# Linear-attention block and gated FFN on one core: later weights behind the last crossbar transpose, first x tiles and K weight halves in turns, four Q units between the halves of the late Gram chunks

**Chip, core, metric.** One core of one Trainium2 chip. The metric is the device time of one execution in microseconds (us). Every execution lists its time and the span of its records; in all runs here the time is the span + 1.7 us. All runs were in the fast state, with a granted TensorE clock of 0.998 to 1.0. Ratios are the mean time of one kernel's fast runs over the mean of the other's fast runs of the same rounds, so they are not quite the ratio of the medians quoted beside them.

## The reference

```python
def reference(A_x, A_wqkv, A_wo, B_x, B_w_gate, B_w_up, B_w_down):
    # x: 1 x 2048 x 576 bf16; wqkv 576 x 1728; 32 heads of 18; FFN width 4608
    xn = _layernorm(x)                               # (x - mean) / sqrt(var + 1e-5)
    q, k, v = split(xn @ wqkv)
    phi = lambda t: jnp.where(t > 0, t + 1, jnp.exp(t)) + 1e-6
    pq, pk = phi(q), phi(k)
    kv = einsum("bhsd,bhse->bhde", pk, v);  z = einsum("bhsd->bhd", pk)
    o = einsum("bhqd,bhde->bhqe", pq, kv) / (einsum("bhqd,bhd->bhq", pq, z)[..., None] + 1e-6)
    ffn = (gelu(xn @ w_gate) * (xn @ w_up)) @ w_down
    return x + o.reshape(B, S, D) @ wo + ffn
```

## The kernel before

The kernel never forms V. It sums the Gram matrix of phi(K) with the normalised x over all 16 token tiles, and multiplies V's weights by it afterwards. For each tile of 128 tokens: VectorE takes statistics and normalises; tiles 0 to 3 are transposed on TensorE, tiles 4 to 15 by a DMA crossbar transpose; TensorE projects K in two halves of 288 columns; ScalarE and VectorE form phi(K); TensorE adds to the Gram chunks. Q units (one of 5 head chunks by 512 tokens) fill in. Chunks 2 and 3 of the Gram matrix wait until chunks 0, 1 and 4 have left PSUM. The order of each engine is the order of a list of (time, step) pairs.

Some words used below. "K 8" or "Gram 15" is that work for tile 8 or 15. A pass is one instruction of VectorE or ScalarE that reads a matmul's result. A bank is one of the eight parts of PSUM (numbers 0 to 7) that the matmuls write. In a row-paired unit two matmuls of 64 rows each start together. The pitch is the even distance between the starts of two pieces of work when TensorE waits for nothing, here 3.05 us from one tile's K to the next; what goes beyond it is called late by the pitch.

```python
    load_x(0, 1)
    load_x(1, 1)
    load_x(2, 2)          # tiles 2 and 3
    load_w(1)             # K weights, all 576 columns
    load_x(4, 2)
    load_x(6, 2)
    load_w(0)             # Q weights
    ...
    def k_bank(n, hf):
        return hf if n == 1 else 5 + hf          # tile 1's halves stand in PSUM banks 0 and 1
    G_A = {0: [(0, ...), (1, ...)], 1: [(2, ...), (3, ...)], 4: [(0, ...), (1, ...), (2, ...)]}   # bank first
    ...
    loads = [lambda n, i=i: load_gu(i // 2, i % 2) for i in range(2 * NWBUF)]   # gate and up blocks
    loads.insert(1, lambda n: load_w(2, 0, 2))                                  # V weights
    loads.insert(3, lambda n: load_w(2, 2, 4))
    todo += [(18.0 + TILE * i, step, 0) for i, step in enumerate(loads)]        # TILE = 2.94
    ...
    for n in range(NS):                       # NS = 16: behind tile 15's Gram
        g_accumulate(n, {2: G_B[2]})
    g_copy(4, G_A, ...); g_copy(0, G_A, ...); g_copy(1, G_A, ...)
    for _, step, n in todo[tail:]:            # the passes of the last Q units
        step(n)
    q_unit(12); ...
```

## Time and profile before

| | before, first profile | before, profile of the first experiment call |
|---|---|---|
| time of that execution | 526.45 | 525.5 |
| span | 524.7 | 523.8 |
| median of the timed runs | 524.73 (524.69 to 524.99) | 524.96 (524.37 to 525.50) |
| crossbar transposes of tiles 8 and 14, issue to landing | 4.52 and 2.60 | 2.61 and 2.59 |
| Gram 15 starts | 54.85 | 53.78 |
| FFN starts | 73.41 | 72.33 |

"Gram 15 starts" is the point up to which the head runs tile by tile; "FFN starts" is the first gate or up matmul. Both can be found in the timeline of TensorE.

### The profile page before, as it was taken

Reading aid. Unit: us, or ns where it says so; the run is one execution under the profiler, and the core shown is the slowest. Engines: PE = TensorE matmul, PEld = TensorE weight load, DVE = VectorE, ACT = ScalarE, POOL = GpSimd, SP = SyncE. Lnnn points to the kernel's source line nnn. Section 1 sums busy time; section 2 is a strip of 40 time slices with the busy share of each in tenths; the row PEclk is TensorE's granted clock in tenths of the full one; section 3 lists DMA queues with packets and bytes.
Section 4 is the critical chain, followed back from the end, with each engine's and each line's share of the span. In section 5 each row is a group of like instructions: output and inputs, shape, how many; then the busy total and the mean of one; then the engine's idle time right before and its main releaser. Section 6 shows DMA issues by size and latency. Waiting matters only on the chain.

```text
span 524.7 us, 10664 instructions
## 1 busy us (share of the span) xinstructions
PE 517.2 (99%) x4502; PEld 315.8 (60%) x4502; DVE 248.4 (47%) x426; ACT 147.9 (28%) x301; POOL 40.1 (8%) x63
## 2 busy tenths in 40 slices
PE   7999999999999999999999999999999999999997
PEld 7767764555577754444577744444777544445775
DVE  7887545977348423333388134333584233333110
ACT  5989563233230012332200033232000123222000
POOL 2012130121001100000011000000011000000000
PEclk9999999999999999999999999999999999999999
DMA  8565009999500035555300065555100355540000
GB/s 262 135 156 119 1 2 240 264 268 265 169 21 24 12 103 158 158 144 158 108 12 13 28 174 143 156 159 151 32 22 12 104 158 157 144 130 1 12 11 24
DMA packets 106443, 57.90 MB, mean 110 GB/s; under 512 B 13402, under 2 KB 105754, under 8 KB 106394
## 3 DMA queue, kind: packets, MB, share of 16 engines
q1 hardware_dynamic: 106394, 57.21, 38.8%
q8 instruction: 35, 0.57, 0.4%
q14 instruction: 14, 0.11, 0.1%
HBM read 52.86 MB, written 2.36 MB: 105 GB/s over the span
## 4 chain that ended last, share of the span: by engine, by line
PE 96%; DMA 2%; ACT 1%; DVE 0%; SPq 0%; issue 0%; DVEq 0%
PE ps_all L318 55%; PE ps_all L664 27%; PE ps_all L669 4%; PE ps_all L294 3%; PE ps_all L250 3%; PE ps_all L347 3%; DMA wqkv_sb<-in_A_wqkv_dram 1%; DMA xnT<-xn 1%; PE ps_all L442 1%; PE ps_all L424 0%; PE ps_all L646 0%; SPq L93 0%; ACT phi_e L270 0%; DVE hT L278 0%; ACT xnT L239 0%; ACT phi_e L274 0%
## 5 line engine op out<-in xcount | busy, mean ns | idle before, releaser
L318 PE MATMUL ps_all<-xnT,wg 64*128 64x512 bf16 x1152 | 273.0, 376 | 0.0
L318 PE MATMUL ps_all<-xnT,wu 64*128 64x512 bf16 x1152 | 271.6, 376 | 0.0
L635 DVE TENSOR_TENSOR hT<-ps_all,gl 128x512 bf16<-128x512 f32 x144 | 99.4, 691 | 161.2 <-ACT gl L634 160.7
L634 ACT ACTIVATE gl<-ps_all 128x512 f32<-128x512 f32 x144 | 86.0, 598 | 312.7 <-PE ps_all L318 295.8
L318 PEld LDWEIGHTS <-wu 64*128 64x128 bf16 x1152 | 108.1, 94 | 66.0 <-SPq L327 0.7
L318 PEld LDWEIGHTS <-wg 64*128 64x128 bf16 x1152 | 108.1, 94 | 65.7 <-issue 0.5
L664 PE MATMUL ps_all<-wd_sb,hT 128*128 128x288 bf16 x1152 | 147.0, 286 | 0.0
L664 PEld LDWEIGHTS <-hT 128*128 128x128 bf16 x1152 | 112.3, 98 | 30.6 <-issue 1.3
L466 DVE RECIPROCAL den_sb<-den_sb 126x128 f32<-126x128 f32 (+1 forms) x80 | 68.3, 911 | 0.5
L672 DVE TENSOR_TENSOR res<-ps_all,x_sb 128x288 bf16<-128x288 f32 x32 | 14.6, 458 | 88.0 <-PE ps_all L669 88.0
L318 PE MATMUL ps_all<-xnT,wr 64*128 64x512 bf16 x288 | 55.7, 376 | 0.0
L469 POOL TENSOR_TENSOR pqT<-pqT,den_sb 126x512 bf16<-126x512 bf16 (+3 forms) x25 | 24.1, 965 | 299.2 <-DVE den_sb L466 276.0
L669 PE MATMUL ps_all<-m_sb,pqT 126*128 126x288 bf16 (+1 forms) x160 | 24.9, 285 | 0.0
L318 PEld LDWEIGHTS <-wr 64*128 64x128 bf16 x288 | 14.6, 94 | 16.7 <-issue 0.7
L250 PE MATMUL ps_all<-wqkv_sb,xnT 128*128 128x288 bf16 x160 | 22.5, 286 | 1.7 <-DMA wqkv_sb<-in_A_wqkv_dram 0.8
L294 PE MATMUL ps_all<-hT,xn 128*128 128x288 bf16 (+4 forms) x176 | 22.4, 276 | 0.0
L294 PEld LDWEIGHTS <-xn 128*128 128x128 bf16 (+1 forms) x176 | 17.5, 102 | 4.3
L250 PEld LDWEIGHTS <-xnT 128*128 128x128 bf16 x160 | 15.3, 98 | 7.6 <-issue 1.3
L393 DVE SCALAR_TENSOR_TENSOR pqT<-ps_all,phi_e 126x512 bf16<-126x512 f32 (+1 forms) x20 | 13.4, 672 | 12.4 <-POOL phi_e L389 12.4
L669 PEld LDWEIGHTS <-pqT 126*128 126x128 bf16 (+1 forms) x160 | 15.5, 97 | 4.1
L347 PE MATMUL ps_all<-xnT,wqkv_sb 128*126 128x512 bf16 (+1 forms) x70 | 17.4, 378 | 0.0
L389 POOL TENSOR_SCALAR phi_e<-phi_e 126x512 f32<-126x512 f32 (+1 forms) x20 | 12.4, 618 | 54.2 <-DVE hT L278 29.8
(63 smaller groups left out, 183.8 us busy)
## 6 DMA issues: line engine op xcount, KB each, us to landing
wg<-in_B_w_gate_dram SPq DMA_DIRECT2D x72, 256.0 KB, 2.9
wu<-in_B_w_up_dram SPq DMA_DIRECT2D x72, 256.0 KB, 3.5
wd_sb<-in_B_w_down_dram SPq DMA_DIRECT2D x12, 432.0 KB, 4.7
wr<-in_B_w_gate_dram SPq DMA_DIRECT2D x72, 32.0 KB, 2.7
wr<-in_B_w_up_dram SPq DMA_DIRECT2D x72, 32.0 KB, 3.1
out_dram<-res SPq DMA_DIRECT2D x15, 144.0 KB, 1.8
wqkv_sb<-in_A_wqkv_dram SPq DMA_DIRECT2D x2, 576.0 KB, 6.0
x_sb<-in_A_x_dram SPq DMA_DIRECT2D x2, 576.0 KB, 7.2
```

The costliest lines, as they stand in the source:

```text
L250: nc.tensor.matmul(ps_all[:, k_bank(n, hf), :HALF], lhsT=xnT[:, kt, n * P:(n + 1) * P], rhs=wqkv_sb[:, kt, D + hf * HALF:D + (hf + 1) * HALF],
L294: nc.tensor.matmul(ps_all[:m, b, col:col + w], lhsT=xn[:, n, j0:j0 + m], rhs=pk[:, n, d0:d0 + w], start=(n == 0 and col == 0), stop=(n == ...
L318: return nc.tensor.matmul(self.outs[i], lhsT=self.lhs(i, rows, kt), rhs=self.rhs(i, rows, kt), start=start, stop=stop, skip_group_check=True,)
L347: nc.tensor.matmul(ps, lhsT=wqkv_sb[:, kt, q0:q0 + rows], rhs=xnT[:, kt, sc * SC:(sc + 1) * SC], start=(kt == 0), stop=(kt == KT - 1),)
L393: nc.vector.scalar_tensor_tensor(out=out_, in0=ps, scalar=0.0, in1=e, op0=ALU.max, op1=ALU.add)
L466: nc.vector.reciprocal(out=d[:, h:h + P], in_=d[:, h:h + P])
L469: nc.gpsimd.tensor_tensor(out=pqT[:rows, c, cols], in0=pqT[:rows, c, cols], in1=d, op=ALU.mult)
L634: nc.scalar.activation(out=gl[:], in_=ps_all[:, b[0], :], func=ACT.Gelu_apprx_tanh)
L635: nc.vector.tensor_tensor(out=hT[:, GUB * k + i, :], in0=ps_all[:, b[1], :], in1=gl[:], op=ALU.mult)
L664: nc.tensor.matmul(acc, lhsT=hT[:, f, j * P:(j + 1) * P], rhs=wd_sb[:, f, hs], start=(f == 0), stop=False,)
L669: nc.tensor.matmul(acc, lhsT=pqT[:rows, c, ts_], rhs=m_sb[:rows, c, hs], start=False, stop=(c == NCH - 1),)
L672: nc.vector.tensor_tensor(out=res[:, hs], in0=acc, in1=x_sb[:, n, hs], op=ALU.add)
```

## The change

Its intent, in three parts. (1) K's first half and x tiles 0 and 1 come first, so that TensorE starts K sooner; the order list of all steps is retuned to that. (2) V, gate and up weights are issued behind the last crossbar transpose, so that no transpose shares the DMA engines with a weight load. (3) The late Gram chunks 2 and 3 are cut into halves, with a Q unit behind each, so that VectorE and ScalarE have time to empty banks while TensorE works.

```diff
 (part 1)
     load_x(0, 1)
     load_x(1, 1)
-    load_x(2, 2)
-    load_w(1)
+    load_wk(0)
+    nc.sync.dma_start(wqkv_sb[0:HP, 4, D:2 * D], A_wqkv[512:576, D:2 * D])
+    load_x(2, 1)
+    load_wk(1)
+    load_x(3, 1)
     load_x(4, 2)
 ... (all 21 lists of times are new; four of them:)
-        (ln_stats, [3.05, 3.99, 6.43, 7.37, 8.65, 10.92, 14.71, 16.48]),
+        (ln_stats, [3.10, 4.04, 6.50, 8.05, 9.69, 12.03, 14.15]),
-        (tp_copy, [x_, 7.00, 9.54, 11.09]),
+        (tp_copy, [x_, 7.05, 10.27, 13.48]),
-        (lambda n: k_sum(n, 0), [9.93, 13.41, 12.85, 15.65, 18.60, 22.03, 24.45, 27.30]),
+        (lambda n: k_sum(n, 0), [9.33, 12.97, 13.43, 16.61, 18.96, 21.58, 24.65]),
-        (lambda n: g_accumulate(n, G_A), [12.97, 14.94, 15.82, 17.80, 23.22, 24.10, 26.08, 29.13]),
+        (lambda n: g_accumulate(n, G_A), [12.54, 13.49, 16.55, 20.83, 21.71, 23.68, 26.74]),
 (part 2)
-    loads = [lambda n, i=i: load_gu(i // 2, i % 2) for i in range(2 * NWBUF)]
-    loads.insert(1, lambda n: load_w(2, 0, 2))
-    loads.insert(3, lambda n: load_w(2, 2, 4))
-    todo += [(18.0 + TILE * i, step, 0) for i, step in enumerate(loads)]
 ... (behind the loop over tiles)
+    load_w(2)
+    for i in range(NWBUF):
+        load_gu(i, 0)
+        load_gu(i, 1)
 (part 3)
-    for n in range(NS):
+    for n in range(NS // 2):
         g_accumulate(n, {2: G_B[2]})
     g_copy(4, G_A, (nc.vector, nc.scalar, nc.vector))
     g_copy(0, G_A, (nc.scalar, nc.vector))
     g_copy(1, G_A, (nc.scalar, nc.vector))
     for _, step, n in todo[tail:]:
         step(n)
-    q_unit(12)
 ...
+    q_whole(12)
+    for n in range(NS // 2, NS):
+        g_accumulate(n, {2: G_B[2]})
+    q_whole(13)
 ... (the same for chunk 3 with units 14 and 19; 15 to 18 stay row-paired)
```

More of the change, by code (lines that the diff above doesn't have):

```diff
@@ L105, with load_w, load_wk @@
     wq_lo = apool.tile([P, D], BF16, name="wq_lo")
-    def load_w(which, k0=0, k1=4):
+    def load_w(which):
         c = slice(which * D, (which + 1) * D)
-        nc.sync.dma_start(
-            wqkv_sb[:, k0:k1, c], A_wqkv[k0 * P:k1 * P, c].rearrange("(kt p) c -> p kt c", p=P))
-        if k1 == 4:
-            nc.sync.dma_start(wqkv_sb[0:HP, 4, c], A_wqkv[512:576, c])
-            if which == 0:
-                nc.sync.dma_start(wq_lo[HP:P, :], A_wqkv[512:576, c])
+        nc.sync.dma_start(wqkv_sb[:, 0:4, c], A_wqkv[0:512, c].rearrange("(kt p) c -> p kt c", p=P))
+        nc.sync.dma_start(wqkv_sb[0:HP, 4, c], A_wqkv[512:576, c])
+        if which == 0:
+            nc.sync.dma_start(wq_lo[HP:P, :], A_wqkv[512:576, c])
+    def load_wk(hf):
+        c = slice(D + hf * HALF, D + (hf + 1) * HALF)
+        nc.sync.dma_start(wqkv_sb[:, 0:4, c], A_wqkv[0:512, c].rearrange("(kt p) c -> p kt c", p=P))
     load_x(0, 1)
     load_x(1, 1)
-    load_x(2, 2)
-    load_w(1)
+    load_wk(0)
[3 more added lines that the diff above has]
+    load_x(3, 1)
     load_x(4, 2)
@@ L304 @@
     SYNC = mybir.DependencyInfo(mybir.DependencyClass.Sync, mybir.DependencyReason.DATA)
-    banks = _Ring([6, 7, 0, 1, 2, 3, 4, 5])
+    banks = _Ring([4, 5, 6, 7, 0, 1, 2, 3])
     class _Unit:
@@ L477 @@
     STEPS = [
-        (ln_stats, [3.05, 3.99, 6.43, 7.37, 8.65, 10.92, 14.71, 16.48]),
-        (ln_rstd, [4.17, 5.11, 7.56, 8.55, 10.38, 13.51, 15.94, 18.79]),
-        (ln_norm, [x_, 5.70, 8.31, 9.59, 11.86, 14.13, 17.42, 20.27]),
-        (ln_dup, [5.61, 6.18, 8.79, 10.07, 12.34, 14.61, 17.90, 20.75]),
-        (transposes, [x_, 6.58, 9.09, 10.37]),
-        (tp_copy, [x_, 7.00, 9.54, 11.09]),
-        (dma_transposes, [x_, x_, x_, x_, 12.58, 14.85, 18.14, 20.99]),
-        (lambda n: k_half(n, 0), [6.87, 9.38, 10.66, 13.72, 16.57, 20.24, 22.61, 25.46]),
@@ L486 @@
-        (lambda n: k_half(n, 1), [7.48, 8.10, 11.27, 14.33, 17.18, 19.63, 22.00, 24.85]),
-        (lambda n: k_relu(n, 0), [7.99, 10.81, 11.93, 14.46, 17.31, 21.11, 23.35, 26.20]),
-        (lambda n: k_relu(n, 1), [8.27, 9.26, 12.67, 15.20, 18.05, 20.37, 22.78, 25.59]),
-        (lambda n: k_exp(n, 0), [8.98, 12.95, 12.39, 14.92, 17.77, 21.57, 23.91, 26.76]),
-        (lambda n: k_exp(n, 1), [10.10, 11.65, 13.23, 15.66, 18.51, 20.83, 23.63, 26.48]),
-        (lambda n: k_sum(n, 0), [9.93, 13.41, 12.85, 15.65, 18.60, 22.03, 24.45, 27.30]),
@@ L492 @@
-        (lambda n: k_sum(n, 1), [10.56, 12.44, 13.77, 16.12, 18.97, 21.29, 24.09, 26.94]),
-        (lambda n: g_accumulate(n, G_A), [12.97, 14.94, 15.82, 17.80, 23.22, 24.10, 26.08, 29.13]),
+        (ln_stats, [3.10, 4.04, 6.50, 8.05, 9.69, 12.03, 14.15]),
+        (ln_rstd, [4.22, 5.16, 7.94, 9.56, 10.83, 14.04, 16.46]),
+        (ln_norm, [x_, 5.75, 8.99, 10.99, 11.69, 15.09, 18.27]),
+        (ln_dup, [5.66, 6.23, 9.47, 11.47, 13.33, 15.57, 18.75]),
+        (transposes, [x_, 6.63, 9.77, 12.25]),
@@ new lines @@
+        (tp_copy, [x_, 7.05, 10.27, 13.48]),
+        (dma_transposes, [x_, x_, x_, x_, 13.57, 15.81, 18.99]),
+        (lambda n: k_half(n, 0), [6.92, 10.06, 11.02, 14.24, 17.30, 19.60, 22.46]),
+        (lambda n: k_half(n, 1), [7.70, 8.31, 11.63, 14.85, 17.91, 20.22, 23.07]),
+        (lambda n: k_relu(n, 0), [7.66, 11.26, 12.00, 14.98, 18.04, 20.45, 23.20]),
+        (lambda n: k_relu(n, 1), [8.44, 9.28, 12.74, 15.72, 18.78, 21.19, 23.94]),
+        (lambda n: k_exp(n, 0), [8.72, 11.72, 12.46, 15.44, 18.50, 20.91, 23.66]),
@@ L494 @@
+        (lambda n: k_exp(n, 1), [9.00, 9.99, 13.20, 16.18, 19.24, 21.65, 24.40]),
+        (lambda n: k_sum(n, 0), [9.33, 12.97, 13.43, 16.61, 18.96, 21.58, 24.65]),
+        (lambda n: k_sum(n, 1), [10.63, 11.33, 13.79, 16.97, 19.70, 22.11, 25.01]),
+        (lambda n: g_accumulate(n, G_A), [12.54, 13.49, 16.55, 20.83, 21.71, 23.68, 26.74]),
     ]
     Q_STEPS = [
-        (q_unit, [11.89, 18.55, 20.85, 26.83, 29.88]),
-        (q_relu, [13.94, 19.76, 22.28, 28.04, 31.09]),
-        (q_exp, [16.37, 24.19, 27.04, 30.10, 33.16]),
@@ L500 @@
-        (q_eps, [17.05, 24.87, 27.72, 30.78, 33.84]),
-        (q_sum, [18.00, 25.75, 28.60, 31.66, 34.72]),
+        (q_unit, [18.52, 15.47, 24.43, 27.49, 30.55, 33.60]),
+        (q_relu, [19.95, 16.89, 25.64, 28.70, 31.76, 34.81]),
+        (q_exp, [21.93, 24.68, 27.73, 31.11, 34.17, 37.22]),
+        (q_eps, [22.61, 25.36, 28.41, 31.79, 34.85, 37.90]),
+        (q_sum, [23.47, 26.31, 29.27, 32.65, 35.71, 38.76]),
     ]
@@ L512 @@
     todo = [*timed(STEPS, NS), *timed(Q_STEPS, NQ)]
-    for n, (na, nb, ta, tb, ca, cb) in enumerate([(4.93, 5.31, 5.31, 5.91, 5.62, 6.16)]):
+    for n, (na, nb, ta, tb, ca, cb) in enumerate([(4.98, 5.36, 5.36, 5.96, 5.67, 6.21)]):
         todo += [
@@ L519 @@
         ]
-    todo += [(t, spin, count) for t, count in [(5.70, 4), (6.23, 3), (6.60, 5), (10.42, 2)]]
-    loads = [lambda n, i=i: load_gu(i // 2, i % 2) for i in range(2 * NWBUF)]
-    loads.insert(1, lambda n: load_w(2, 0, 2))
-    loads.insert(3, lambda n: load_w(2, 2, 4))
-    todo += [(18.0 + TILE * i, step, 0) for i, step in enumerate(loads)]
+    todo += [(t, spin, count) for t, count in [(5.70, 4), (6.23, 3), (6.64, 4), (8.95, 4), (12.26, 3)]]
     todo.sort(key=lambda x: x[0])
@@ L546, in g_copy, with q_whole @@
                 nc.vector.tensor_scalar_add(out=out_, in0=in_, scalar1=eps)
-    for n in range(NS):
+    load_w(2)
+    for i in range(NWBUF):
+        load_gu(i, 0)
+        load_gu(i, 1)
+    def q_whole(i):
+        q_unit(i)
+        for step in (q_relu, q_exp, q_eps, q_sum):
+            step(i)
+    for n in range(NS // 2):
         g_accumulate(n, {2: G_B[2]})
@@ L554 @@
         step(n)
-    q_unit(12)
-    for step in (q_relu, q_exp, q_eps, q_sum):
-        step(12)
-    for n in range(NS):
+    q_whole(12)
+    for n in range(NS // 2, NS):
+        g_accumulate(n, {2: G_B[2]})
+    q_whole(13)
+    g_copy(2, G_B, (nc.scalar, nc.vector))
+    for n in range(NS // 2):
         g_accumulate(n, {3: G_B[3]})
-    g_copy(2, G_B, (nc.scalar, nc.vector))
+    q_whole(14)
+    for n in range(NS // 2, NS):
+        g_accumulate(n, {3: G_B[3]})
+    q_unit(19)
     g_copy(3, G_B, (nc.scalar, nc.vector))
-    q_unit(13)
     z_stage(2, 3)
@@ L565 @@
     for step in (q_relu, q_exp, q_eps, q_sum):
-        step(13)
-    q_banks = _Ring(list(range(6)))
-    prev = None
-    for units in [[15, 16], [17, 18], [14, 19], None]:
-        if units:
-            u = q_pair(units)
-            u.p1()
-        if prev:
-            prev[1].p2()
-            for step in (q_relu, q_exp, q_eps, q_sum):
-                for i in prev[0]:
-                    step(i)
-        prev = (units, u)
+        step(19)
+    q_banks = _Ring(list(range(4)))
+    pairs = [q_pair([15, 16]), q_pair([17, 18])]
+    for u in pairs:
+        u.p1()
+    for u, units in zip(pairs, ([15, 16], [17, 18])):
+        u.p2()
+        for step in (q_relu, q_exp, q_eps, q_sum):
+            for i in units:
+                step(i)
     scales = []
```

## The prediction

> **What bounds the kernel now.** I first read the page's busy shares: TensorE is busy 517.2 of 524.7 us, so a change that only reorders work has about 7.5 us to win in all. I then asked the waits of TensorE for the whole span.
>
> ```profile
> PE 517.2 (99%) x4502; PEld 315.8 (60%) x4502; DVE 248.4 (47%) x426; ACT 147.9 (28%) x301; POOL 40.1 (8%) x63
> ```
> ```profile
> PE ps_all L138 <- POOL ident masks.py:199: 1.4, 1, 1.4
> PE ps_all L250 <- DMA wqkv_sb<-in_A_wqkv_dram: 0.8, 1, 0.8
> PE ps_all L250 <- DMA xnT<-xn: 0.7, 1, 0.7
> PE ps_all L236 <- ACT xnT L239: 0.6, 1, 0.6
> PE ps_all L250 <- DVE hT L278: 0.2, 1, 0.2
> ```
>
> These five are all the waits that TensorE has. The first (the start) and the output's tail are untouched by the change. Four waits, 2.3 us, lie in the attention head, before the FFN begins at about 73.4 us. The chain of work that ended last (start, duration, what) shows where:
>
> ```profile
> 2.20 6.00 DMA wqkv_sb<-in_A_wqkv_dram
> 8.20 0.04 issue
> 8.24 1.40 PE ps_all L250 x10
> ...
> 22.75 1.08 PE ps_all L347 x5
> 23.83 1.33 PE ps_all L250 x10
> ...
> 25.84 4.52 DMA xnT<-xn
> 30.36 0.05 issue
> 30.41 1.40 PE ps_all L250 x10
> ...
> 54.99 4.77 PE ps_all L294 x39
> 59.76 1.08 PE ps_all L347 x5
> 60.84 4.00 PE ps_all L294 x32
> 64.84 1.08 PE ps_all L347 x5
> ```
>
> The reader is to see: the K projection (L250) starts only when all 576 KB of the K weights have landed, at 8.20; one crossbar transpose, issued at 25.84 between two weight loads, took 4.52 us and stopped TensorE; from 30.41 to 65.92 TensorE runs without a gap (K 1.23, Gram L294 0.75, Q L347 1.08 per tile). From 67.60 on it is the FFN and its like, whose instructions and order the change leaves alone apart from bank numbers.
>
> **What the Trainium skill says.** "TensorE: Matmul & The Clock Gate", section "Back-to-back issue gap", gives N/2.4 + 2.5 ns between warm matmuls: 122.5 ns for N=288 and 215.8 for 512. The trace agrees: 10 K matmuls per 1.23 us, 5 Q matmuls per 1.08 us; so I count TensorE by issue pitch, not by the modelled 286 and 378 ns. "DMA: Bandwidth & Descriptors", section "Queues, rings and completion order", says that completion is not FIFO per issuing engine, as the engines run through their rings separately. The trace agrees in part: when the K weights landed (8.20), about 1.74 MB had moved (the rates of the first 24 slices of 0 to 14 us), though only 1.18 MB stood in the queue up to their end. So a transfer lands 1 to 2 us after its bytes' turn. The same page's "Specifications" put full rate at 512 B and above; the K halves have 576 B runs, so they stay above, but the gate and up blocks with 512 B runs moved at 264 to 268 GB/s with the engines 95% busy and more, where the first loads with 1152 B and up reached 370, so smaller runs cost something here.
>
> **Part 1, first x tiles and K halves in turns.** By issue and landing times in the profile (and the bytes in front): x0 landed at 3.0, x1 at 3.5 (294 KB in decimal bytes), x2 with x3 at 5.4 (589 KB), the K weights at 8.20 (1180 KB), their tail at 8.5. New queue: x0, x1, K half 0, tail, x2, K half 1, x3. Estimates from that scale: half 0 (589 KB) at 5.7, tail 6.0, x2 6.5, half 1 (1105 KB) 8.0, x3 (1253 KB) 8.4. Half 0's matmuls can start when tile 0's transposed copy is there: its second part ended at 6.95 on VectorE, so about 7.25 instead of 8.24. But x3 comes 3 us later than before (8.4 for 5.4), and in VectorE's new order the statistics of tile 3 still stand ahead of the normalisation of tile 2. So that starts at 8.4 + 1.0 (statistics and aggregate, from 7.84 to 8.84 in the trace) = 9.35, where it was 8.76. Then by the trace's durations: norm 0.38, pad copy 0.24 on GpSimd, transposes 0.44 and copy 0.69 with handoffs bring tile 2's K to 11.1. Walking on in the new order, tile 3's transposes come at 12.4, Gram 0 and 1 end at about 14.5, K 3, Q, Gram 2 at 17.6, K 4 and Q at 19.9, K 5, Gram 3 and 4 at 22.65, when K 6 starts. From there to Gram 15 is 10 K (12.28) + 10 Gram (7.45) + 10 Q (10.8) = 30.5: start at 53.2. Before it was 54.85. Gain 1.65.
>
> **Part 2, later weights behind the last transpose.** This is within that 1.65: after its K 6 (23.67) the kernel before has 30.2 us of work to Gram 15 and took 31.2; the 1.0 is the stall at 30.41 (0.7 idle, 0.87 by issue pitch) and crumbs. With the crossbar alone, a transpose lands in the 2.6 us that the profile shows for most, within the 3.5 us that the schedule leaves. The remaining 0.65 of the gain is the earlier start. The moved loads, 0.65 MB of V weights and 2.36 MB of gate and up blocks, need about 11.5 us at 264 GB/s from about 48 us on: V weights there at 52 (needed at 66), the last block at 61 (first needed at 73). Hidden.
>
> **Part 3, four Q units between Gram halves.** Units 14 and 19 leave a row-paired unit (18 matmuls, 1.95 us by the FFN's 0.108 pitch) and run singly (2 x 1.08): +0.2. What matters more is a bank. Q units alternate between banks 4 and 7, so unit 12 needs unit 10's last VectorE pass. Before, unit 12 came after all 16 tiles of Gram chunk 2. Now it comes after 8, that is 0.75 + 2.0 = 2.75 us after Gram 15 begins. And in VectorE's new order unit 10's pass no longer stands ahead of the Gram evacuations but behind them. In the timeline before (start, us, engine, line):
>
> ```profile
> 55.59 0.69 DVE L393 SCALAR_TENSOR_TENSOR pqT<-ps_all,phi_e 126x512 bf16<-126x512 f32 x1 [0.79 <-POOL phi_e L389]
> 56.20 0.14 DVE L539 TENSOR_SCALAR eps_sum<-ps_all 65x1 f32<-65x1 f32 x1
> ...
> 57.80 0.52 DVE L546 TENSOR_SCALAR g_sb<-ps_all,eps_sum 128x288 bf16<-128x288 f32 x1
> ```
>
> The evacuations took 56.20 to 58.32 = 2.12. In the new order they start 1.0 after Gram 15 begins, end at 3.1, unit 10's pass (0.69) ends at 3.8, unit 12 starts at 3.85: a new stall of 3.85 - 2.75 = 1.1 us. The other three units I walked the same way: unit 13 finds bank 7 free with 1.8 us to spare, 14 with 2 us, 19 with 2; the last Gram copy ends 0.6 us ahead of the KV matmuls that read it. At the FFN's start the before kernel lost 0.5 (714 row matmuls in 77.65, at 0.1081 each 77.16) to relays behind DMA issues on SyncE; the new kernel keeps that order, so I count nothing.
>
> **Sum.** -1.65 + 0.2 + 1.1 = -0.35: 524.73 - 0.35 = about 524.4.
>
> **Rivals.** (a) The bank stall doesn't come, or less: if VectorE's evacuations ran quicker or the pass came in between. Nothing in the order speaks for it; it would make 523.3. (b) x3 lands later than 8.4, since the 576 B runs cost more: each 1 us shifts the whole head by as much, up to the stall-free start of before; with 9.4 the time is 525.3. For it: the K weights took 2.8 us after x3 in the trace for 590 KB, slower than any other early load. (c) The head is held by TensorE alone from 7.25 on: work of 14.3 us to K 6 would put it at 21.6 and the time at 523.3; against it, the chain through tiles 2 and 3 on three engines. (d) The burst of loads at 48 to 61 us delays something: no reader waits then, and the loads are the same in bytes.
>
> **Range and chances.** Each term is below 2 us, so 2% (10.5 us) either way needs a failure of a sort that I don't see: same 0.98. Runs agree to 0.3 us; (b) and (a) or (c) set the ends: 523.2 to 525.4.
>
> **What would show it.** First K matmul near 7.25 and a wait on the second half until about 8; tile 2's normalisation later than before, at 9.3; no transpose over 3 us among tiles 6 to 15 and no wait of TensorE on one; Gram 15 at 53.2; a wait of about 1.1 us of Q (L352) on VectorE at about 56; none at the three others. I am wrong if that wait is missing, or if x3 lands a microsecond from 8.4, or if the FFN's first microseconds change by more than 0.3.

## The result

The changed kernel takes 527.99 us (527.72 to 528.26, 4 runs) where before takes 524.71 (524.56 to 524.99, 4 runs): ratio 1.0062 [1.0044, 1.0079]. That is 3.3 us more, within 2% as predicted, but outside the range of 523.2 to 525.4, and the direction is wrong. The waits of TensorE over the whole span of the changed kernel (columns: what waited, for what, us in total, times, longest):

```profile
PE ps_all L143 <- POOL ident masks.py:199: 1.4, 1, 1.4
PE ps_all L352 <- DVE pqT L398: 0.8, 1, 0.8
PE ps_all L255 <- DMA xnT<-xn: 0.7, 2, 0.4
PE ps_all L255 <- ACT xnT L244: 0.6, 1, 0.6
PE ps_all L299 <- DVE hT L283: 0.5, 1, 0.5
PE ps_all L255 <- DMA wqkv_sb<-in_A_wqkv_dram: 0.5, 1, 0.5
PE ps_all L241 <- DVE xn L226: 0.4, 2, 0.2
```

L255 is K, L299 Gram, L352 Q; the lines have moved by five since before, where they were L250, L294 and L347, and move again with the edits below. Beside the list of before: the one wait on a transpose (0.7) has become two, Gram waits 0.5 for VectorE, Q waits 0.8. The chain of work that ended last (start, duration, what):

```profile
25.96 4.16 DMA xnT<-xn
30.16 0.80 PE ps_all L255 x5
...
44.87 4.13 DMA xnT<-xn
49.04 1.40 PE ps_all L255 x10
...
55.32 0.77 PE ps_all L299 x7
56.30 0.70 DVE g_sb L546 x2
57.11 0.52 DVE g_sb L546
57.73 0.52 DVE g_sb L546
58.24 0.61 DVE pqT L398
58.90 1.24 PE ps_all L352 x5
```

Three places show in it. Two transposes took over 4 us, those of tiles 8 and 14, although no weight load was in the queue. The third is the bank wait of Q unit 12, which stands there as predicted: Gram evacuations on VectorE, unit 10's pass behind them, unit 12.

The waits of the *unchanged* kernel in the profile of the first experiment are the other half of the story:

```profile
PE ps_all L138 <- POOL ident masks.py:199: 1.4, 1, 1.4
PE ps_all L250 <- DMA wqkv_sb<-in_A_wqkv_dram: 1.1, 1, 1.1
PE ps_all L236 <- ACT xnT L239: 0.6, 1, 0.6
PE ps_all L250 <- DVE hT L278: 0.2, 1, 0.2
```

No wait on a transpose at all, although the DMA traffic around tile 8's transpose (25.6 to 30.2 us of this profile) holds a load of V weights, as in the first profile, and instruction packets too (what they are follows below):

```profile
q8 instruction: 1, 0.02, 2.4%
q14 instruction: 1, 0.01, 0.9%
wqkv_sb<-in_A_wqkv_dram SPq DMA_DIRECT2D x1, 288.0 KB, 4.4
xnT<-xn SPq DMA_TRANSPOSE x2, 2.6
```

The stall of tile 8 that the prediction removed is in one execution of before and not in another. Where the 2.5 us between the profiles of the same call (spans 523.8 and 526.3) lie:

| | before | changed | difference |
|---|---|---|---|
| K of tile 6 starts | 23.47 | 23.73 | +0.26 |
| work moved behind that point (a Gram 0.75 done sooner, a Q 1.08 later) | | | +0.33 |
| K 8 behind K 7, beyond the even pitch of 3.05 | 0 | 0.50 | +0.50 |
| K 14 behind K 13, beyond 3.05 | 0 | 0.64 | +0.64 |
| Gram 15 starts (sum of the above, and crumbs of -0.09) | 53.78 | 55.42 | +1.64 |
| Gram 15 to the FFN's start | 18.55 | 19.76 | +1.21 |
| FFN to the end | 451.43 | 451.12 | -0.31 |

The first row is not a chance of this pair. K 6 starts at 22.95 to 23.67 in the five profiles with before's order of the front (b4_best, which has its own, not counted) and at 23.33 to 23.94 in the nine with the change's order (without those that have a4's edit or sooner transposes). The means, 23.37 and 23.62, are 0.25 apart.

### The profile page after: what moved, and what is told of

The parts are those of the page before. It is cut to its first block, busy times and chain, and to the rows that moved or that the text cites. A ratio compares the mean times of both kernels' runs of the same rounds, so it can differ in the third digit from the quotient of the medians.

```text
span 526.2 us, 10656 instructions
## 1 busy us (share of the span) xinstructions
PE 517.5 (98%) x4498; PEld 313.8 (60%) x4498; DVE 248.5 (47%) x426; ACT 149.2 (28%) x301; POOL 40.0 (8%) x63
## 4 chain that ended last, share of the span: by engine, by line
PE 91%; ACT 4%; DMA 2%; DVE 1%; SPq 0%; issue 0%; DVEq 0%; ACTq 0%
PE ps_all L323 54%; PE ps_all L676 27%; PE ps_all L681 4%; PE ps_all L299 2%; DMA xnT<-xn 2%; PE ps_all L352 1%; PE ps_all L255 1%; ACT phi_e L279 1%; ACT phi_e L275 1%; DMA wqkv_sb<-in_A_wqkv_dram 1%; PE ps_all L447 1%; ACT phi_e L386 0%; ACT phi_e L390 0%; DVE pqT L398 0%; DVE g_sb L546 0%
## 5 line engine op out<-in xcount | busy, mean ns | idle before, releaser
L255 PE MATMUL ps_all<-wqkv_sb,xnT 128*128 128x288 bf16 x160 | 22.5, 286 | 1.8 <-DMA xnT<-xn 0.7
L299 PE MATMUL ps_all<-hT,xn 128*128 128x288 bf16 (+4 forms) x176 | 22.9, 275 | 0.5 <-DVE hT L283 0.5
L352 PE MATMUL ps_all<-xnT,wqkv_sb 128*126 128x512 bf16 (+1 forms) x80 | 19.8, 378 | 0.8 <-DVE pqT L398 0.8
L299 PEld LDWEIGHTS <-xn 128*128 128x128 bf16 (+1 forms) x176 | 17.5, 101 | 5.1 <-issue 0.6
L255 PEld LDWEIGHTS <-xnT 128*128 128x128 bf16 x160 | 15.2, 98 | 8.1 <-DMA xnT<-xn 1.7
```

The lines of the kernel that those rows point to most:

```text
L255: nc.tensor.matmul(ps_all[:, k_bank(n, hf), :HALF], lhsT=xnT[:, kt, n * P:(n + 1) * P], rhs=wqkv_sb[:, kt, D + hf * HALF:D + (hf + 1) * HALF],
L299: nc.tensor.matmul(ps_all[:m, b, col:col + w], lhsT=xn[:, n, j0:j0 + m], rhs=pk[:, n, d0:d0 + w], start=(n == 0 and col == 0), stop=(n == ...
L352: nc.tensor.matmul(ps, lhsT=wqkv_sb[:, kt, q0:q0 + rows], rhs=xnT[:, kt, sc * SC:(sc + 1) * SC], start=(kt == 0), stop=(kt == KT - 1),)
```

## What a slow transpose looks like

The DMA traffic of the changed kernel in the stretch of tile 8's slow transpose (25.9 to 30.2 us; the next transpose begins in it):

```profile
q1 hardware_dynamic: 793, 0.19, 22.8%
q8 instruction: 1, 0.02, 1.3%
xnT<-xn SPq DMA_TRANSPOSE x2, 3.4
```

The columns are packets, MB and share of the 16 engines; the last line has the median from issue to landing, here of 4.2 and 2.6. There is no weight load; the only other traffic is one packet of 0.02 MB of the queue "instruction". The page counts 35 such packets, 0.57 MB, over the span: 16 KB each. The single DMA records give the times: the transpose was issued at 25.96; 15 of its 16 engines had reported by 2.57 us after that; the fetch began 2.11 us after the issue, and the sixteenth engine reported at 4.16. The slow transpose of the unchanged kernel's first profile (4.52, fetch 2.00 after the issue) looks the same: 15 engines by 2.59, the last at 4.52. So its weight loads need not be to blame.

The Trainium skill, "Runtime: NRT & Kernel Launch", section "Instruction fetch mechanics", says that an engine's instructions are refilled in 16 KiB blocks of 256 by a DMA queue that the sequencer drives itself, and that the cost is mostly hidden. Size and count agree: the page gives TensorE 4498 matmuls and 4498 weight loads, 35.1 blocks of 256, and 35 packets of this queue (q8) were seen. A second instruction queue, q14, has 14 packets of 8 KB, which this count leaves to other engines. Before the experiments, the statement that the fetch delays the transpose was a reading, no more.

## The experiments

18 runs, each beside runs of the kernel before on the same chip. "Slow" is a transpose over 4 us. "Tail" is Gram 15 to the FFN's start.

| run | what | median us | ratio to before | K 6 / Gram 15 | tail | tile 8 / 14 |
|---|---|---|---|---|---|---|
| b0_before | before, unchanged | 524.96 | 0.999 [0.9978, 1.0003] | 23.47 / 53.78 | 18.55 | 2.61 / 2.59 |
| a0_after | changed, unchanged | 527.90 | 1.0047 [1.0035, 1.006] | 23.73 / 55.42 | 19.76 | 4.16 / 4.22 |
| a1_pass | changed, unit 10's pass first | 526.74 | 1.0027 [1.0015, 1.004] | 23.48 / 55.06 | 18.77 | 4.12 / 4.14 |
| b1_loads | before + part 2 | 525.13 | 0.9994 [0.9981, 1.0008] | 22.95 / 54.63 | 18.56 | 4.34 / 4.65 |
| a2_spins | changed, 8 warm-up matmuls fewer | 527.43 | 1.0045 [1.0028, 1.0062] | 23.60 / 54.89 | 19.76 | 2.58 / 4.33 |
| a3_tail | changed - part 3 | 526.88 | 1.0037 [1.0022, 1.0052] | 23.75 / 55.56 | 18.55 | 4.21 / 4.28 |
| a4_bank0 | changed, tile 1's pass sooner | 527.50 | 1.0051 [1.0036, 1.0066] | 23.19 / 54.88 | 19.76 | 4.15 / 4.22 |
| b3_first | before + part 1's loads | 525.00 | 1.0003 [0.9988, 1.0018] | 23.25 / 53.55 | 18.56 | 2.61 / 2.58 |
| a7_decoy | changed, a load behind 8 and 14 | 528.23 | 1.0063 [1.0049, 1.0076] | 23.33 / 55.04 | 19.75 | 4.23 / 4.15 |
| a8_all | a1 + a4 + a7 | 526.80 | 1.0035 [1.0022, 1.0047] | 23.21 / 55.19 | 18.78 | 4.29 / 4.37 |
| b4_best | before + loads, order mended | 526.57 | 1.0031 [1.0017, 1.0044] | 24.68 / 55.86 | 18.55 | 4.52 / 2.58 |
| a9_spread | changed - part 2 | 528.34 | 1.0063 [1.005, 1.0077] | 23.81 / 55.79 | 19.76 | 4.31 / 4.36 |
| a10_mended | a9 + a1 + a4 | 526.46 | 1.003 [1.0017, 1.0042] | 23.01 / 54.88 | 18.77 | 4.29 / 4.25 |
| a11_front | before + part 1 with its order | 526.75 | 1.0038 [1.0025, 1.005] | 23.35 / 55.19 | 18.56 | 4.29 / 4.23 |
| a12_wide | changed, 42 TensorE instructions fewer | 527.87 | 1.0057 [1.0043, 1.0071] | 23.94 / 55.56 | 19.76 | tiles 9 / 15: 4.20 / 4.29 |
| a14_earlyonly | changed, transposes issued sooner | 529.51 | 1.0084 [1.0071, 1.0097] | 25.12 / 56.73 | 19.76 | none over 3.14 |
| a13_early | a10, transposes issued sooner | 527.74 | 1.0052 [1.0039, 1.0064] | 24.80 / 56.40 | 18.77 | none over 3.61 |
| b5_early | before, transposes issued sooner | 525.81 | 1.0015 [1.0001, 1.0029] | 23.51 / 54.85 | 18.56 | tiles 9 / 15: 3.44 / 4.08 |

The kernels with one chip: b0, a0, a1, b1 (before 525.34); a2, a3, a4, b3 (before 525.12); a7, a8, b4 (524.81); a9 to a12 (524.87); a13, a14, b5 (524.99). All gave correct results.

**Both kernels again (b0_before, a0_after).** No edit.

> The kernel before, unchanged, against itself. It asks how far one profiled span can be trusted: the recorded times of before are 524.7 us, but the one profiled execution of it that I predicted from took 526.45 us with a span of 524.7, while the changed kernel's times (528.0) are 1.7 us over its spans (526.2). If the time is always the span plus 1.7, the usual span of before is 523.0 and the profile that I read is of an execution that was 1.7 us slower than the usual one; then this run's span should be near 523.0 and its trace should lack some wait of the first one. If the profile itself adds 1.7, the span should be 524.7 again. Ratio 1.000 within 0.001 either way.

> The changed kernel, unchanged. Ratio to before 1.006 again if the difference is the kernel's own. In the trace: Q unit 12 waits 0.8 to 1.1 us for VectorE near 58 us; two crossbar transposes of over 4 us, at 26 and 45 us, each with a 16 KB instruction fetch in flight and 15 of its 16 engines finished by 2.6 us. If those two are chance, they are at other places or missing.

The difference repeats on another chip (2.5 us between the two profiled runs, 2.9 by the medians). In the changed kernel the slow transposes come back at the same two tiles; in before neither is slow. The execution of before without the stall took 525.50, no less than the median of all of before's runs on that chip (525.34). So the stall that the prediction took from the first profile can hardly be part of a usual execution of before; it isn't shown run by run, as the timed runs left no trace. Of the 1.7 us by which the first profile was slow, the stall is 0.87 and a later start of K 0.2 (8.24 for 8.04); the rest isn't placed.

**The pass of unit 10 ahead of the Gram evacuations (a1_pass).**

```diff
+    ahead = [x for x in todo[tail:] if x[1] is q_sum and x[2] == 10]
+    for _, step, n in ahead:
+        step(n)
     for n in range(NS // 2):
         g_accumulate(n, {2: G_B[2]})
 ... (and left out of the passes behind the evacuations)
```

> The changed kernel with unit 10's last VectorE pass put ahead of the Gram evacuations, as it stood before the change. Theory (bank 4 is released late): the wait of Q unit 12 on VectorE goes, and the time falls by 0.8 to 1.0 us against the changed kernel, ratio to it 0.998. Rival (the evacuations themselves come to sit on the path): the 0.54 us that they start later come back at unit 13 or at the KV matmuls, and the time falls by less than 0.5 us.

VectorE's timeline in the changed kernel (start, duration, engine, line) and then in this one:

```profile
57.73 0.52 DVE L546 TENSOR_SCALAR g_sb<-ps_all,eps_sum 128x288 bf16<-128x288 f32 x1
58.16 0.68 DVE L398 SCALAR_TENSOR_TENSOR pqT<-ps_all,phi_e 126x512 bf16<-126x512 f32 x1
```
```profile
55.85 0.69 DVE L398 SCALAR_TENSOR_TENSOR pqT<-ps_all,phi_e 126x512 bf16<-126x512 f32 x1 [0.82 <-POOL phi_e L394]
56.45 0.14 DVE L539 TENSOR_SCALAR eps_sum<-ps_all 65x1 f32<-65x1 f32 x1
```

The pass, of the same length, comes 2.3 us sooner, no wait of Q is left in the profile, the tail is 18.77 instead of 19.76, and the time falls by 1.16 (527.90 to 526.74). Of this the tail is 0.99. The term of the prediction that named this stall, 1.1 us, held.

**Part 2 alone on the kernel before (b1_loads).** The `loads` list removed; V, gate and up loads issued behind the loop over tiles.

> The kernel before with the V weights and the first gate and up blocks issued behind the last crossbar transpose, and nothing else changed. Theory A (weight loads slow the transposes, the change's intent): no transpose over 3 us, the wait of K tile 8 goes, time down 0.7 to 0.9 us. Theory B (what slows a transpose is an instruction fetch on one DMA engine): tile 8's transpose still takes over 4 us at the fetch near 28 us, tile 14's may do so too at the fetch near 47 us, which fell on a weight load before, and the time is the same within 0.3 us or up to 0.6 us longer.

With the crossbar alone, both transposes were slow, 4.34 and 4.65, and TensorE's list of waits has one line for the two:

```profile
PE ps_all L250 <- DMA xnT<-xn: 1.0, 2, 0.5
```

That refutes the prediction's cause: a transpose is slow without weight loads, as it was quick beside them in b0. The time is not above before's (its profile fell on its slowest run, 525.95; the others are 524.85 to 525.59), so the stalls may not be in each of its runs.

**Eight warm-up matmuls fewer (a2_spins).** `[(5.70, 4), (6.23, 3), (6.64, 4), (8.95, 4), (12.26, 3)]` became `[(5.70, 4), (6.23, 3), (12.26, 3)]`.

> The changed kernel without 8 of its idle-filling 128x128 matmuls (two groups of 4), so that the TensorE program is 8 matmuls shorter and its 16 KB instruction fetches come about 1 us later against the transposes, at about 29.0 and 47.8 us, when the transposes of tiles 8 and 14 should already have landed. Theory (a fetch in the data phase of a transpose holds one of 16 engines): no transpose over 3 us, no wait of K tiles 8 and 14 on a transpose, time down by about 1.0 us to 0.998 of the changed kernel (526.9 for 527.9). Rival (those transposes are slow for another reason, such as what tiles 8 and 14 do): both stay over 4 us and the time is the same within 0.3. The removed matmuls filled waits, so by themselves they give at most 0.2 us.

A miss in the mechanism: the fetches did not come a microsecond later (28.20 and 46.41). Tile 8's transpose had the fetch 2.20 us after the issue and was not slow; tile 14's at 2.00 and was (4.33). Gram 15 came 0.5 us sooner than in a0.

**Part 3 undone (a3_tail).** The tail and the bank order of before in the changed kernel.

> The changed kernel with its third part undone: both late Gram chunks whole again, Q units 12 and 13 after them, three row-paired units, the old bank order. Theory: the wait of Q unit 12 on VectorE (0.8 by the profile, 1.0 by issue pitch) and the 0.2 us of single units go: 1.1 to 1.2 us less than the changed kernel, 526.7 for 527.9. Rival (the part does earn something at the FFN's start, where fewer paired units leave ScalarE free sooner): less than 0.8 us less.

The tail is back at 18.55. On the same chip it takes 526.88 beside 527.43 and 527.50 of the two with part 3; that is less than the 1.2 us of the tail, since its Gram 15 came 0.7 later than theirs in its profile. (Those two have edits of their own; the plain changed kernel was not run on this chip.) Both slow transposes stay.

**Tile 1's half read sooner (a4_bank0).** In the list of `k_sum(n, 0)`, 12.97 became 12.02.

> The changed kernel with one VectorE pass moved: tile 1's first half is summed before Gram 0 is issued, and before the statistics of tile 5. In both kernels that pass stood after Gram 0, which writes the same PSUM bank 0, so that it waited for Gram 0 and Gram 1 waited for it (0.47 us near 14.6). Theory: that wait goes, and everything from K tile 3 on comes 0.4 to 0.6 us sooner: 527.3 to 527.5 for 527.9. Rival (tile 3's copy on ScalarE, which ends near 14.9, is the true bound for K tile 3): less than 0.2 us.

In the changed kernel, Gram 0 and 1 stand ahead of K 3 on TensorE:

```profile
13.26 0.91 PE L299 MATMUL ps_all<-hT,xn 128*128 128x288 bf16 x7
14.63 0.91 PE L299 MATMUL ps_all<-hT,xn 128*128 128x288 bf16 x7 [0.47 <-DVE hT L283]
15.38 0.41 PE L255 MATMUL ps_all<-wqkv_sb,xnT 128*128 128x288 bf16 x2
```

Gram 1 waits for VectorE's pass on tile 1's first half, and that pass waits for Gram 0, because tile 1's half stands in bank 0, which Gram 0 writes, and the list puts the pass behind Gram 0. (In both kernels the pass therefore stands behind the write of that bank in program order. I read that as a slip that the comparison's tolerance hides; no run tested it for itself.) With the edit the wait is gone and K 3 starts at 15.01 instead of 15.56; the profile's span is 525.8 against 526.3 of a0. The ratio doesn't resolve it.

**Part 1's loads alone (b3_first).** The new load order and `load_wk`, nothing else.

> The kernel before with the first part's loads alone (K weight halves and single x tiles in turns), all orders as before. Theory: the first K matmuls start near 6.8 instead of 8.1, but x tile 3 lands near 8.4 instead of 5.4, tile 2's normalisation waits for its statistics, and Gram 15 starts no sooner: the time is the same within 0.3 us or up to 0.8 us longer (525.3 to 526.1 beside 525.3). Rival (the K weights are what holds the head): up to 1.0 us less.

K started at 6.80 instead of 8.04, and the time is that of before. VectorE shows why (its timeline in this run):

```profile
8.44 0.82 DVE L219 BATCH_NORM_STATS2 stats<-x_sb 128x6 f32<-128x288 bf16 x2 [0.60 <-DMA x_sb<-in_A_x_dram]
9.42 0.38 DVE L228 TENSOR_SCALAR xn<-x_sb,mv,rstd 128x576 bf16<-128x576 bf16 x1
```

The statistics of tile 3 stand ahead of the normalisation of tile 2, and x3 now comes later. K 3 starts at 14.79, Gram 15 at 53.55: 0.2 us sooner than in b0, no more.

**One load behind each of the two transposes (a7_decoy), and three repairs at once (a8_all).**

```diff
+    todo += [(24.88, lambda n: load_gu(0, n), 0), (42.52, lambda n: load_gu(0, n), 1)]
     todo.sort(key=lambda x: x[0])
 ... (the loads behind the loop then begin with block 1)
```

a8 has this edit with those of a1 and a4.

> The changed kernel with one gate load put back right behind the crossbar transpose of tile 8 and one up load right behind that of tile 14; the other later loads stay behind the last transpose. Theory (an instruction fetch that starts 2.0 to 2.3 us after the issue of a transpose with an empty queue behind it holds the sixteenth engine's share of it, 4.1 to 4.3 us instead of 2.6; with a load queued behind, the load takes the delay): both transposes are back at 2.6 to 3, the two K waits of 0.34 and 0.40 us are gone, Gram 15 starts 0.5 to 1.0 us sooner than in the changed kernel (55.2 to 55.4 there), and the time falls by 0.5 to 1.0 us, 527.9 to 526.9-527.4. Rival (the fetch's place against the transpose decides alone, the load behind it doesn't matter): both stay at 4.1 or more and the time stays within 0.2 us of 527.9. A load put there can itself do harm: then other transposes get longer than 3 us.

> The changed kernel with three repairs at once: the pass of unit 10 ahead of the Gram evacuations, the half of tile 1 read 1 us sooner, and the two loads put behind the transposes of tiles 8 and 14. If the causes found one by one are separate and are all there is, the gains add: 1.16 for the pass, 0.3 to 0.5 for the half, and what the two loads give alone in the same call (0.5 to 1.0 if the theory of the fetch holds): 525.4 to 526.0, so within 1 us of the kernel before (525.2), with Gram 15 at 54.2 to 54.5 against 53.8 before. Rival (something else in the tail or the FFN costs too, or one repair moves the fetch or another wait into the place of the removed one): 526.3 or more.

The theory of the decoy fell: both transposes stayed at 4.15 to 4.37 with a load right behind. a8 comes 1.43 us below a7 on the same chip, somewhat less than the 1.5 to 1.7 that the two repairs' own gains make (1.16, and for the half the expected 0.3 to 0.5, which a4's ratio doesn't resolve), and 2.0 us above before.

**Part 1's loads in an order made for them (b4_best).**

```diff
-        (ln_stats, [3.05, 3.99, 6.43, 7.37,
+        (ln_stats, [3.05, 3.99, 6.43, 8.40,
-        (transposes, [x_, 6.58, 9.09, 10.37]),
+        (transposes, [x_, 6.58, 9.09, 11.00]),
 ... (rstd, norm, dup and copy of tile 3 behind that of tile 2; k_sum(1, 0) 13.41 to 12.90)
```

> The kernel before with the change's first loads alone, and with the order of the engines mended for them: the statistics of tile 3 after the normalisation of tile 2, the transposes of tile 3 between the K halves of tile 2, and the half of tile 1 read before Gram 0 writes its bank. With the loads alone the normalisation of tile 2 came at 9.42 because VectorE waited 0.60 us for tile 3. Theory (the early loads are worth something only with an order that uses them): that wait is gone, the normalisation of tile 2 is at about 8.5, the K of tile 3 starts 0.3 to 0.6 us sooner than the 14.79 of the loads alone, and the time is 524.4 to 524.8 beside 525.1 of before. Rival (the front is bound by TensorE's own work up to tile 3, or the time saved there is lost in the following waits for K weights or transposes): K of tile 3 within 0.2 us of 14.8 and the time within 0.2 us of before.

A miss: K 3 at 16.50, 1.7 later than in b3. TensorE waits 1.4 us in K for a VectorE pass (`hT`) that my order had put too late. Mending one engine's order by hand made another's wrong; it says nothing against early loads.

**Part 2 undone (a9_spread), and then the other two mended (a10_mended), and part 1 with its order alone (a11_front).** In a9 the `loads` list is back, from 18.85 on. a10 adds the edits of a1 and a4. a11 is a9 with the tail of before.

> The changed kernel with its second part undone: V, gate and up loads one behind each transpose from tile 6 on, as in the kernel before. So far a transpose of tile 8 or 14 took over 4 us in 17 of 18 cases of kernels that keep these loads behind the last transpose, and in 2 of 8 of kernels that spread them. Theory: with them spread most of these stalls go; Gram 15 starts 0.5 to 1.0 us sooner than the 55.2 to 55.4 of the changed kernel, and the time is 526.9 to 527.5 where the changed kernel has 527.9 to 528.2. Rival (the stalls come from the front's order, whatever the loads): both transposes stay over 4.1 us and the time at 527.9 or more.

> The changed kernel with the loads spread as before, the pass of unit 10 ahead of the Gram evacuations, and the half of tile 1 read 1 us sooner: the second part undone and the other two mended. If the three repairs of 524.81+2 that fell short at 526.8 did so because the front's gain was taken back by the two transpose stalls, this one comes to 525.3 to 526.0, Gram 15 at 53.9 to 54.5 (53.8 in the kernel before, 55.2 with the three repairs). Rival (something else in the changed kernel costs 1 to 2 us): 526.5 or more.

> The kernel before with the first part and its order of the front alone (later loads spread, tail of before). The first loads without that order gave 525.0, like the kernel before (525.1). Theory from the trace of the changed kernel: the order costs 0.3 to 0.5 us (the half of tile 1 read after Gram 0 wrote its bank, ScalarE's small ops ahead of tile 2's copy), less 0.33 us of work that comes later: Gram 15 at 54.0 to 54.6, time 525.1 to 525.8, and with the changed tail 527.0 less about 1.2, the same. Rival (the front is what costs most of the 3 us): 526.5 or more.

The loads' place makes no difference: a9 has both slow transposes and 528.34. The rivals were right in all three. a10 is 1.88 below a9, where the tail gives 0.99 and Gram 15 comes 0.91 sooner. The pass holds here too; of the 0.91, 0.35 is there at K 2 already (11.49 for 11.84), ahead of what the half can change, and 0.46 comes between K 2 and K 3, as in a4 beside a0 (0.47). What is left of a10 against before is 1.6 us by the medians. In its profile K 8 and K 14 come 0.65 and 0.68 us late by the pitch, and the rest of its tail is 0.22 longer than before's, which is the two single units. 1.33 + 0.22 = 1.55. (The 0.33 of moved work and the K 6 that is 0.46 sooner than b0's nearly cancel in this account; the span of the one profile is 0.96 above b0's.) In a10 and a11 the list of waits puts the wait of K 8 down to VectorE's statistics (0.5), which K doesn't read; K 8 starts 0.04 to 0.05 us after the transpose landed. a11, 1.9 us above before with the tail and the loads of before, has its K 6 no later than before (23.35 beside 23.47), and then the same two stalls, 0.63 and 0.66. So, by this account, the front's new order costs through them.

**Fewer instructions in the same time (a12_wide).** 28 of the 38 warm-up matmuls of 128 columns became 7 of 512 columns, so TensorE has 42 instructions (matmuls and weight loads) fewer ahead of the first tile; a tile has 44.

> The changed kernel with 28 of its 38 warm-up matmuls of 128 columns replaced by 7 of 512 columns: the same TensorE time, 21 matmuls and as many weight loads fewer. If the slow transposes follow the fetch of TensorE's instructions, which comes every 256 of them: the fetches come about one tile (44 instructions, 3.05 us) later, and the transposes of tiles 9 and 15 are the slow ones, those of 8 and 14 take 2.6; the time stays within 0.5 us of the changed kernel. Rival (bound to these tiles, by their place in the buffer or by what runs beside them): 8 and 14 stay slow. A third way is that the fetches don't move (as when 8 matmuls were taken away): then TensorE's count isn't what places them, and the cause of their place stays open.

The fetches moved by a tile, from 28.25 and 47.26 (a0) to 31.15 and 50.42, and the slow transposes with them. The chain of this run:

```profile
29.21 4.20 DMA xnT<-xn
33.41 0.05 issue
33.46 0.80 PE ps_all L258 x5
```

Tiles 8 and 14 follow at the pitch of 3.05; K 9 is 0.37 late, K 15 0.72. This settles what delays the transpose: the fetch of TensorE's instructions, not the tile, its buffer, or a load.

**Transposes issued sooner (a14_earlyonly, a13_early, b5_early).** VectorE's normalisation of a tile moved ahead of the statistics of its period; in a14 no other engine's order changes.

```diff
-        (ln_norm, [x_, 5.75, 8.99, 10.99, 11.69, 15.09, 18.27]),
+        (ln_norm, [x_, 5.75, 8.99, 10.99, 11.69, 15.09, 16.50]),
 ... (ln_dup 18.75 to 16.90, dma_transposes 18.99 to 17.12; in b5 also the rstd, 18.79 to 18.20)
```

> The changed kernel with VectorE's normalisation of tiles 6 to 15 moved behind the K sums of the period before, ahead of the statistics; the order of every other engine is the same. The transposes are issued about 1.4 us sooner, so K has 5.1 us for them instead of 3.7. Theory: transposes may still take 4.2 us, but TensorE waits for none of them; K of tiles 8 and 14 follow at the even pitch of 3.05; Gram 15 starts 0.9 to 1.3 us sooner than in the changed kernel (55.2 to 55.4, so 54.0 to 54.4), and the time falls from 527.9-528.3 to 526.7-527.2. Rival (the pace is set by something else, or VectorE's new order makes TensorE wait for sums): Gram 15 at 55 or later, 527.7 or more.

> The same early normalisation in the kernel that has the loads spread as before, the pass of unit 10 ahead and the half of tile 1 read sooner (526.46 without it, Gram 15 at 54.88, waits of 0.65 and 0.68 by the pitch on tiles 8 and 14). Theory: both waits go, Gram 15 at 53.5 to 53.8, time 525.0 to 525.5, the time of the kernel before within 0.6 us: then wait of unit 12, half of tile 1 and the two stalls are the whole difference. Rival (another cost of 1 us or more is left): 526 or more.

> The kernel before with the reciprocal deviation and the normalisation of tiles 7 to 15 moved ahead of the statistics of the period, so that the transposes are issued 1 to 1.4 us sooner. Theory: the usual run of before has no such stall, but some of its runs have one or two (its times spread from 524.0 to 526.3); with the margin the slow runs go: median 524.3 to 524.8 and a spread under 1 us. Rival (the spread of before has another cause): median within 0.2 us of before and the same spread; or, if VectorE's new order delays a K sum, slower.

Of the seven waits of TensorE in a14 up to 82 us, the three that are longest after that of the start:

```profile
PE ps_all L352 <- DVE pqT L398: 1.3, 2, 0.8
PE ps_all L255 <- DVE hT L283: 1.3, 2, 0.7
PE ps_all L255 <- ACT xnT L244: 0.7, 1, 0.7
```

TensorE waits for no transpose any more, but for VectorE's sums, which now stand behind a normalisation that waits for ScalarE. All three were slower than without the edit, so the rivals were right about the time, and none of these kernels shows what the head would take without the two stalls. That the stalls are the cost rests on the account by the pitch, in a10 and a11, not on a run in which they alone are gone. The nearest to one are the two profiles of the unchanged kernel: the one with tile 8's stall, 0.87 by the pitch, has a span 0.98 longer, with K's start 0.2 later. None of the runs beats the kernel before clear of noise. b5's runs spread less (0.67 in 5 runs, where before has 1.5 in 9), as its theory said, but about a higher median.

**The fetch and the transpose, over all profiles.** Tiles 8 to 15, and packets of TensorE's queue (q8), with the beginning of the fetch counted from the transpose's issue:

| fetch begins after | cases | transpose lands after |
|---|---|---|
| 0.47 to 0.57 | 2 | 3.0 to 3.1 |
| 0.89 to 1.06 | 3 | 3.4 to 3.6 |
| 1.51 | 1 | 4.1, all 16 engines late |
| 1.94 to 2.19 | 20 | 4.1 to 4.5, every one; 15 engines by 2.7 |
| 2.20 to 2.50 | 13 | 4.2 to 4.65 in 7, 2.6 in 6 |
| 2.59 | 1 | 2.6 |

b0 and b3 lie at 2.25 to 2.59, where it didn't hit; all profiles with the front's new order and the transposes at their old place lie at 1.94 to 2.31, and 23 of the 24 transposes met were slow. Tile 5, which the table leaves out, says the same of the other instruction queue: in the first profile of before and in those of b0, b1, b3, b4 and b5 a packet of q14 began 2.06 to 2.14 us after its issue, 15 engines had reported by 2.62, and it landed at 3.4 to 3.8. So it is not a matter of TensorE's stream in particular, nor of tiles 8 and 14.

Some tenths of a microsecond decide. What sets these tenths stays open: 42 instructions fewer moved it by a tile (a12), but 16 fewer (a2) did not move it, so the count alone doesn't place it.

## Why the prediction was wrong, point by point

**The failed step: part 2, "the 1.0 is the stall at 30.41", and with it "with the crossbar alone, a transpose lands in the 2.6 us".** The prediction saw a slow transpose between two weight loads and made the loads its cause, and counted the stall's removal as 1.0 us of gain. The cause was the instruction fetch (a12 and the table for it; b0, b1 and a9 against the loads). And most likely the gain was not there to be had: the span of the profile it was read from, 524.7, stands for 526.45 us, 1.7 more than the median that the sum was applied to, and b0, without the stall, was no faster than before's other runs. The page and the times were both in hand, and the two were not compared. In place of -1.0 stands +1.14 (0.50 for tile 8, 0.64 for tile 14).

**Part 1, "the remaining 0.65 of the gain is the earlier start": mis-sized, and of the wrong sign.** Against b0, the front is a loss of 0.26 + 0.33 = 0.6 us. The DMA half of the walk was right: the first K came at 6.78 (7.25 predicted), x3 landed at 8.37 (8.4), tile 2's normalisation was at 9.38 (9.35). The engine half was too short. K 2 came at 11.58 for 11.1, as a relu, the two steps of tile 3's deviation and an exponential stand ahead of tile 2's copy on ScalarE, which began at 10.85; then Gram 1 waited 0.47 for a bank that the walk didn't check. K 6 came at 23.55 for 22.65. b3 shows that early loads without an order that uses them give nothing.

**Part 3: right.** The wait of unit 12 was predicted at 1.1; it is 0.82 in the waits, 1.0 by the pitch, and its repair gave 1.16. No wait at units 13, 14 and 19, as predicted. The two single units cost 0.2 (tail of a1 18.77 for 18.55). From Gram 15 to the FFN it is 19.76, where before's 18.56 and the two predicted terms make 19.86.

**Rivals.** (b), x3 late, did not come. (a) and (c) would have been gains. Nor did (d), harm from the burst of loads: with the loads behind and the old tail, Gram 15 to the FFN takes 18.55 (a3), as in before. No rival held that the stall of tile 8 might be a matter of chance, though the one transpose of over 4 us among the ten between 20 and 52 us was the thing to ask about.

**Two readings that no sum hangs on.** In the stretch of the gate and up blocks (91.8 to 131.2 us of the first profile) the DMA engines are 91 to 93% busy, not 95; and the 370 GB/s of the first loads is the best of slices of 0.35 us, while 264 to 268 are means of 13 us. The mean from 4 to 14 us is 325. And the page cited for the pace of matmuls gives N/2.4 + 2.5 for an isolated matmul; for a stream of weight loads and matmuls it gives about 131 ns at N=512. Here five Q matmuls in a stream took 1.08 us, 216 ns each, so the measurement decides, and it is the measurement that the prediction counted by.

**Sum.** Predicted -1.65 + 0.2 + 1.1 = -0.35. Measured, between the profiles: +0.6 (front) + 1.14 (tiles 8 and 14) + 1.2 (tail: 0.2 + 1.0) - 0.31 (the FFN, whose instructions and order the change leaves alone; why it is shorter stays open) and crumbs = 2.5.

## What to carry to other kernels

Before subtracting a stall, check that the profiled execution is a usual one: span plus the fixed difference to the time, against the median of the timed runs; a profile 1.7 us slow can hold just the stall that is to be removed. A transfer that lands late without company is worth a look at its single engines: one of sixteen late, with a 16 KB packet of the instruction queue beside it, is no matter of load order. And where a buffer is freed by a pass on another engine, look where that engine's order puts the pass: that paper walk gave the one term that came out within 0.1 us.

## What the Trainium skill lacked or had wrong

- "Runtime: NRT & Kernel Launch", section "Instruction fetch mechanics", calls the cost of crossing a 16 KiB block mostly hidden. For TensorE's own stream no wait was seen here, but the fetch shares the DMA engines with data: a crossbar transpose that lands after 2.6 us took 4.1 to 4.65 in 27 of the 33 cases in which a fetch began 1.94 to 2.50 us after its issue, and in the profiles of this account K came 0.37 to 0.87 us late for it by the pitch. The page doesn't say so.
- "DMA: Bandwidth & Descriptors", section "Why a DMA increments its semaphore by 16 and not by 1", explains that only all 16 increments mean that a transfer has landed; the trace agrees (15 of 16 engines at 2.57 us, the last at 4.16, and K 0.04 us later). Section "Queues, rings and completion order" says that an increment follows every earlier write of its engine, across its queues, which no run here tests, and counts the refill of instructions among the queue rows that the DMA engines serve in turn, so the sharing as such is told there. The page has no figure for what one foreign packet of 16 KB costs: 1.6 us here.
- No page that I read has the time from issue to landing of a crossbar transpose of 128 x 640 bf16 within SBUF: 2.6 us, in all profiles, with nothing beside it.
